# Held-back output steps after the first exponential burst, and the place of the row-sum product, in a fused attention and SwiGLU kernel

## The chip, the cores and the metric

The kernel runs on one core of one Trainium2 chip. Its time is device time in microseconds (us), the median of three executions. The profile is of one further execution. The engines are PE (TensorE, matrix products), DVE (VectorE), ACT (ScalarE), POOL (GpSimd) and SP (SyncE, which here only issues DMAs). Each of them works through its own instructions in the order in which the program has them, and semaphores hold an instruction back until what it needs is there.

## What is computed

Four batches of 12416 rows of 128 channels pass an attention over 32 inducing points, and then a gated feed-forward of width 1536:

```python
def mab(q, kv):
    s = scale * (q @ kv.transpose(0, 2, 1))
    s = s - s.max(-1, keepdims=True)
    a = np.exp(s)
    a /= a.sum(-1, keepdims=True) + 1e-09
    return a @ kv
h = mab(I, x)            # 32 rows per batch, over all 12416 rows of x
attn = mab(x, h)         # every row of x, over the 32 rows of h
g = attn @ w_gate
out = (g * sigmoid(g) * (attn @ w_val)) @ w_out
```

## The kernel before

**Columns, tiles and slots.** A batch is cut into 25 columns of 480 or 512 rows (`COLS`), and a column's feed-forward into 12 tiles of 128 hidden units (t = 0 to 11). Each batch thus has 300 slots, one per tile. In a slot the program issues a **front** (L694 and L695: two matmuls of up to 512 columns into two PSUM tiles of the six in `ps_gv`), the gate on ACT (L700, silu), the product with the value on DVE (L708), and the **split** of tiles that are due (L716 and L718: a rounded copy `h_hi`, nearly always on ACT, and the rest `h_lo`, on POOL, or on DVE for t = 1, 5 and 9). It ends with **backs** (L737 to L739: three matmuls into an accumulator `o`, of which two exist), of tiles that were fronted some slots earlier. L739 is the one that reads `h_lo`. A split is due one slot after its front where t is 1, 5 or 9, three slots after where t is 0, 4 or 8, else two. Below, "front 43" is that of slot 43 of the first batch, and "tile 40" the tile fronted in slot 40.

**Held-back steps.** `pend` lists the tiles fronted but not yet backed. After each slot, backs are issued while `pend` is longer than `ahead`. `ahead` rises by a sixth a slot up to 11 (`RAMP`, `HI`) until the last burst of the batch. In the second and third batch it rises evenly up to their first burst.

**Bursts.** In a burst slot, ACT gets a long run of exponentials with two loads of its function table around them, and PE gets all backs that the fall of `ahead` sets free: `ahead` drops to `SKEW`, which is 6, and in the first batch to 5. All tiles that wait for their split are then rounded on DVE. The first batch has a burst at slot 36 (`E0`: exponentials of its own second attention), one at slot 131 (`nxt.e1`: of the next batch's first attention) and a third later.

**The next batch's attention** is laid into the slots of the current batch by `plan`, as steps with a due slot. Steps are taken in the order of their due slots, and a step whose `acc` lists the t of the oldest held tile waits (as do all behind it). Such are the score steps `s1` (due at slots 82 and 103 here), `max_b` (110) and `hacc`, since they take one of the two `o` buffers. From slot 131 on come: the exponentials; in slot 134 three `hacc` (L323, 84 matmul passes into one `o` tile, the "hacc visit"); then `h_a` (L331, the product of the row sums), and in the next slot `h_r` and `h_b` on DVE (L335 to L337, three tiny operations on the sums, and L341, which reads the `o` tile of the visit and sets it free). The steps of the current batch's own second attention (`post`: on DVE L207, L208, L467, L475 and a rounding, on POOL L471 and L484) and leftovers of the start-up (on POOL L457) lie in fixed slots between.

The lines that decide how many steps are held:

```python
if slot < first_burst:
    ahead += (HI - ahead) / (first_burst - slot)
else:
    ahead = min(ahead + 1 / RAMP, HI) if slot < last_burst else max(ahead - 1 / RAMP, SKEW)
if slot in bursts:
    ahead = SKEW - (b == 0)
while len(pend) > ahead:
```

Of the kernel before, what the change touches and what calls it, by code (L numbers as in the profile page):

```python
# [40 lines left out]
NT = DFF // P  # L41
# [9 lines left out]
SKEW = 6  # L51

S2O = list(range(NCH - NXT, NCH)) + list(range(NCH - NXT))
NXN = 3
# [7 lines left out]
E0 = 36  # L62
# [49 lines left out]
def induced_set_attention_then_swiglu(ctx: ExitStack, tc: tile.TileContext, xt, xn, ind, wgv, wo, out):  # L112
# [58 lines left out]
    class Piece:  # L171
# [23 lines left out]
        def add(self):  # L195
            nc.gpsimd.tensor_add(out=self.w.bitcast(I32), in0=self.t.bitcast(I32), in1=self.lw.bitcast(I32))  # L196
# [365 lines left out]
    def plan(st, p):  # L562

        f, s = st.f, []

        def add(slot, step, *args):
            def go():
                f[step](*args)


            go.step = step
            go.acc = (NT - 1, 0, 1) + (2,) * (step not in ("max_b", "h_c")) if step in ("s1", "max_b", "hacc", "h_c", "s2") else ()
            s.append((slot, go))

        def blocks(q):
            return CH0[q], CH0[q] + CH[q]

        last = p["S1"][0] + p["S1"][1] * (NCH - 1)
        v1 = last - 3 * p["S1"][1]
        for q in range(NCH):  # L580
            add(p["LX"][0] + p["LX"][1] * q if q < NXT else v1 + 1 + 3 * (q - NXT), "load_xt", q)

            add(v1 if q < NXT else last, "s1", q, q not in (0, NXT))
        mb = last + p["MX"]
        add(last + 2, "max_a"), add(mb, "max_b")
        e1 = mb + p["E1"]
        for q in range(NXN):
            add(e1 - p["LN"][0] + p["LN"][1] * q, "load_xn", q)
            add(e1, "exp1_part", q)
            add(e1, "eT", q)  # L590
            add(e1 + p["HA"][q], "hacc", q, (0, NXN - 1))
        add(e1 + p["HA"][NXN - 1], "h_a")
        add(e1 + p["HA"][NXN - 1] + 1, "h_r")
        add(e1 + p["HA"][NXN - 1] + 1, "h_b")
        add(e1, "exp1_part", NXN, NCH - 1)
        for q in range(NXN, NCH):
            k = NXN + (q - NXN | 1)
            at = e1 + p["HB"][0] + p["HB"][1] * (k - NXN)
            add(max(at - p["HC"][0] - k + q, e1 + 1 + (p["HB"][0] + p["HB"][1] if q == NCH - 1 else p["HA"][0])), "load_xn", q)
            add(at - p["HC"][1] + 1 - k + q, "eT", q)  # L600
            add(at, "hacc", q, (k - 1, k))
        add(at + 1, "h_s")
        hn = at + p["HD"]
        add(hn, "h_c")
        for i, q in enumerate(S2O):
            k = i % NXT
            at = hn + 4 + p["H2"] * (NXT - 1) if i < NXT else hn + p["H2"] * (NCH - 1)
            add(at, "s2", *blocks(q), i not in (0, NXT))
            if i + NXT < NCH:
                add(at + 1, "load_xt", S2O[i + NXT])  # L610
            d = 2 if i < NXT else 1
            add(at + 1 + d * k, "s2_max", *blocks(q))
            add(at + 3 + (d + 1) * k, "s2_sub", *blocks(q))
        e2 = at + 4 + p["E2"]
        add(e2, "exp2")
        st.e1, st.bursts = e1, {e1, e2}
        for i in range(2):
            add(e2 + p["PR"][0], "proj_round", i)
            for k in range(NG * NG):
                add(e2 + p["PR"][i] + 3 + k * p["PQ"], "proj_spread", i, k // NG, k % NG)  # L620
        for q in range(NF):
            first = [u for u, (p, j) in enumerate(COLS) if p == q][0]
            s += post(st, q, nc.gpsimd, SLOTS + NT * (first - NST) + 2, SLOTS)
        return sorted(s, key=lambda x: x[0])
# [5 lines left out]
    with tc.tile_pool(name="xt0", bufs=NCH - NXT) as xt0, tc.tile_pool(name="xn0", bufs=NCH - NXN) as xn0:  # L630
# [17 lines left out]
        def run(token):  # L648
# [13 lines left out]
            e1=lambda q: f["exp1_part"](q, g=int(q >= GA)), eT=f["eT"], hq=f["hacc2"], fs=f["rescale"], su=f["sums"],  # L662
# [102 lines left out]
    for b in range(B):  # L765
        nxt = attention(b + 1, (one, oneb)[(b + 1) % 2]) if b + 1 < B else None
        if nxt is not None:
            nxt.steps = plan(nxt, PA if b == 0 else PB)
            if b == 0:
                cur.steps.append((nxt.e1, lambda: run(f"e2:52:{NTB}")))  # L770
                for q in range(2, NF):
                    base = NT * (1 + NG * (q - 1) - NST) + 2
                    base = max(base, E0 + 6) if q < 4 else max(base, nxt.e1 + 4)
                    cur.steps += post(cur, q, nc.gpsimd, base)
                cur.steps.sort(key=lambda x: x[0])
        bursts = (nxt.bursts if nxt is not None else set()) | ({E0} if b == 0 else set())
        last_burst = max(bursts, default=0)
        first_burst = min(bursts, default=0) if b else 0
        for slot in range(NT if b == 0 else 0, SLOTS):
            c, t = slot // NT, slot % NT  # L780
            u = front(cur, b, c, t)
            gate(u)
            value(u)
            left = (B - b) * SLOTS - slot
            u.cast = same if t in CAST and left > 1 else nc.scalar.copy
            u.last, u.near = left == 1, left < 3
            u.due = slot + (1 if t in DVE_TILES or left < 5 or b == 0 and slot < 2 * NT else 3 if t + 1 in DVE_TILES else 2)
            if slot in bursts:
                for w in wait + [u]:
                    w.cast = same  # L790
            for w in [w for w in wait if w.due <= slot]:
                now(w)
            wait.append(u)
            pend.append(u)
            if slot in bursts:
                while wait:
                    now(wait[0])
            for a in (cur, nxt):
                while a is not None and a.steps and a.steps[0][0] <= slot:

                    if pend and pend[0].t in getattr(a.steps[0][1], "acc", ()):
                        break
                    step = getattr(a.steps[0][1], "step", "")
                    if step == "h_c" and slot < a.hb + 3:
                        break
                    if step == "h_s":
                        a.hb = slot
                    a.steps.pop(0)[1]()
            if slot < first_burst:
                ahead += (HI - ahead) / (first_burst - slot)  # L810
            else:
                ahead = min(ahead + 1 / RAMP, HI) if slot < last_burst else max(ahead - 1 / RAMP, SKEW)
            if slot in bursts:
                ahead = SKEW - (b == 0)
            while len(pend) > ahead:
                if pend[0] in wait:
                    now(pend[0])
                back(pend.pop(0))
        if nxt is not None:
            nxt.steps = [(at - SLOTS, f) for at, f in nxt.steps]  # L820
        for u in wait:
            u.due -= SLOTS
        cur = nxt
# [45 lines left out]
```

## Time and profile before

| | us |
|---|---|
| median of three executions | 1379.59 |
| lowest and highest of the three | 1379.53, 1379.64 |
| the profiled execution | 1379.63 |
| its span, from the first to the last instruction | 1377.8 |
| PE busy, by the page | 1368.3 |
| ACT busy | 1241.5 |
| DVE busy | 1195.4 |
| POOL busy | 1180.8 |

The busy time of PE holds pipelined matmuls whose records overlap, and short waits disappear in it. Distances from start to start show what PE does: a matmul of 512 columns has a record of 380 ns, and the next one starts 216 ns later.

### The profile page before, as it was taken

Reading aid. Unit: us, or ns where it says so; the run is one execution under the profiler, and the core shown is the slowest. Engines: PE = TensorE matmul, PEld = TensorE weight load, DVE = VectorE, ACT = ScalarE, POOL = GpSimd, SP = SyncE. Lnnn points to the kernel's source line nnn. Section 1 sums busy time; section 2 is a strip of 40 time slices with the busy share of each in tenths; the row PEclk is TensorE's granted clock in tenths of the full one; section 3 lists DMA queues with packets and bytes.
Section 4 is the critical chain, followed back from the end, with each engine's and each line's share of the span. In section 5 each row is a group of like instructions: output and inputs, shape, how many; then the busy total and the mean of one; then the engine's idle time right before and its main releaser. Section 6 shows DMA issues by size and latency. Waiting matters only on the chain.

```text
span 1377.8 us, 25215 instructions
## 1 busy us (share of the span) xinstructions
PE 1368.3 (99%) x7459; PEld 1182.2 (86%) x7459; DVE 1195.4 (87%) x2088; ACT 1241.5 (90%) x2380; POOL 1180.8 (86%) x994
## 2 busy tenths in 40 slices
PE   9999999999999999999999999999999999999998
PEld 6578788889988887899998888789999888889998
DVE  6889879988988889888898888988888888888887
ACT  4989898889998888899999889799999999999998
POOL 1689868889998878899898878889989989989987
PEclk9999999999999999999999999999999999999999
DMA  9224424312144343221123523321111111111110
GB/s 365 85 85 144 147 82 142 125 46 73 41 126 154 107 142 111 64 58 44 44 69 119 178 77 112 121 72 53 44 37 45 39 47 39 39 45 38 42 44 22
DMA packets 50680, 119.49 MB, mean 87 GB/s; under 512 B 11376, under 2 KB 28272, under 8 KB 50544
## 3 DMA queue, kind: packets, MB, share of 16 engines
q1 hardware_dynamic: 50544, 117.90, 26.1%
q8 instruction: 59, 0.97, 0.3%
q14 instruction: 77, 0.63, 0.2%
HBM read 62.54 MB, written 25.43 MB: 64 GB/s over the span
## 4 chain that ended last, share of the span: by engine, by line
PE 96%; ACT 2%; DVE 1%; DMA 1%; issue 0%; SPq 0%; DVEq 0%; ACTq 0%
PE o L737 18%; PE gv L694 18%; PE gv L695 18%; PE o L738 18%; PE o L739 18%; PE gv L275 2%; PE o L323 1%; PE o L275 1%; DMA xt_sb<-xt 1%; ACT silu L700 1%; PE o L734 0%; PE gv L424 0%; PE gv L267 0%; DVE eT L313 0%; ACT xn_sb L184 0%
## 5 line engine op out<-in xcount | busy, mean ns | idle before, releaser
L718 POOL TENSOR_TENSOR h_lo<-h,h_hi 128x512 fp32r<-128x512 f32 (+1 forms) x889 | 1089.8, 1255 | 149.1 <-ACT h_hi L716 107.9
L700 ACT ACTIVATE silu<-gv 128x512 f32<-128x512 f32 (+1 forms) x1200 | 707.1, 590 | 105.2 <-PE gv L694 72.4
L708 DVE TENSOR_TENSOR h<-gv,silu 128x512 f32<-128x512 f32 (+1 forms) x891 | 588.9, 665 | 90.4 <-PE o L738 50.6
L716 ACT CAST h_hi<-h 128x512 fp32r<-128x512 f32 (+1 forms) x778 | 470.5, 605 | 0.5 <-DVE h L708 0.5
L694 PE MATMUL gv<-stack,tw 128*128 128x512 f32 (+1 forms) x1200 | 452.4, 377 | 1.6 <-DVE stack L544 1.0
L695 PE MATMUL gv<-stack,tw 128*128 128x512 f32 (+1 forms) x1200 | 448.3, 374 | 0.2 <-ACT silu L700 0.2
L737 PE MATMUL o<-h_hi,wo_lo 128*128 128x512 f32 (+1 forms) x1188 | 445.4, 375 | 0.4 <-DVE hn L341 0.4
L739 PE MATMUL o<-h_lo,wo_hi 128*128 128x512 f32 (+1 forms) x1188 | 443.0, 373 | 0.0
L738 PE MATMUL o<-h_hi,wo_hi 128*128 128x512 f32 (+1 forms) x1188 | 442.8, 373 | 0.0
L708 DVE TENSOR_TENSOR gv<-gv,silu 128x512 f32<-128x512 f32 (+1 forms) x297 | 202.4, 682 | 68.4 <-PE o L738 46.0
L694 PEld LDWEIGHTS gv<-stack,tw 128*128 128x128 f32 x1200 | 226.8, 189 | 34.6 <-ACT tw L416 3.1
L737 PEld LDWEIGHTS o<-h_hi,wo_lo 128*128 128x128 f32 x1188 | 224.5, 189 | 34.1 <-issue 10.6
L695 PEld LDWEIGHTS gv<-stack,tw 128*128 128x128 f32 x1200 | 226.7, 189 | 30.3 <-ACT silu L700 4.0
L739 PEld LDWEIGHTS o<-h_lo,wo_hi 128*128 128x128 f32 x1188 | 224.5, 189 | 24.8 <-POOL h_lo L718 0.5
L738 PEld LDWEIGHTS o<-h_hi,wo_hi 128*128 128x128 f32 x1188 | 224.6, 189 | 23.4
L718 DVE TENSOR_TENSOR h_lo<-gv,h_hi 128x512 fp32r<-128x512 f32 (+1 forms) x297 | 197.3, 664 | 0.8
L716 ACT CAST h_hi<-gv 128x512 fp32r<-128x512 f32 (+1 forms) x295 | 168.7, 572 | 7.5 <-DVE gv L708 7.0
L211 DVE TENSOR_REDUCE h_hi<-h 128x512 fp32r<-128x512 f32 (+1 forms) x113 | 73.7, 661 | 0.0
L748 DVE COPY ob<-o 128x512 f32<-128x512 f32 (+1 forms) x99 | 65.7, 664 | 0.2 <-PE o L739 0.2
L484 POOL TENSOR_TENSOR a_lo<-aT,a_hi 128x480 fp32r<-128x480 f32 (+2 forms) x26 | 30.1, 1159 | 0.0
L196 POOL TENSOR_TENSOR wgv_sb<-s_all 128x512 int32<-128x512 int32 x2 | 2.9, 1492 | 28.8 <-ACT s_all L184 28.8
L471 POOL TENSOR_TENSOR s_all<-s_all,sm 128x512 f32<-128x512 f32 (+2 forms) x27 | 26.1, 965 | 0.0
(156 smaller groups left out, 480.9 us busy)
## 6 DMA issues: line engine op xcount, KB each, us to landing
xt_sb<-xt SPq DMA_DIRECT2D x32, 896.0 KB, 5.0
xn_sb<-xn SPq DMA_DIRECT2D x18, 896.0 KB, 5.6
out<-ob SPq DMA_DIRECT2D x52, 256.0 KB, 2.0
out<-ob SPq DMA_DIRECT2D x48, 240.0 KB, 2.0
stack<-a_hi SPq DMA_DIRECT2D x96, 64.0 KB, 2.0
stack<-a_lo SPq DMA_DIRECT2D x96, 64.0 KB, 2.0
stack<-a_hi SPq DMA_DIRECT2D x96, 60.0 KB, 2.0
stack<-a_lo SPq DMA_DIRECT2D x96, 60.0 KB, 2.0
```

Source lines behind the costliest of these rows:

```text
L211: nc.vector.tensor_reduce(out=out, in_=in_.unsqueeze(2), op=ALU.max, axis=AX.X)
L275: nc.tensor.matmul(out=ps[32 * j:32 * j + 32, 32 * (lo - b0):32 * (hi - b0)], lhsT=lhsT, rhs=st.xt[q][:, lo - CH0[q]:hi - CH0[q], j, :], s ...
L694: nc.tensor.matmul(out=u.g[:, :n], lhsT=st.w[:, wcol(0, t)], rhs=rhs, start=True, stop=True)
L695: nc.tensor.matmul(out=u.v[:, :n], lhsT=st.w[:, wcol(1, t)], rhs=rhs, start=True, stop=True)
L700: nc.scalar.activation(out=u.s[:, :u.n], in_=u.g[:, :u.n], func=AF.Silu)
L708: nc.vector.tensor_mul(out=u.h[:, :n], in0=u.v[:, :n], in1=u.s[:, :n])
L716: u.cast(out=u.hi[:, :n], in_=u.h[:, :n])
L718: eng.tensor_sub(out=u.lo[:, :n], in0=u.h[:, :n], in1=u.hi[:, :n].bitcast(F32))
L737: nc.tensor.matmul(out=o[:, :n], lhsT=wo_lo[:, ws], rhs=hi, start=(t == 0), stop=False)
L738: nc.tensor.matmul(out=o[:, :n], lhsT=wo_hi[:, ws], rhs=hi, start=False, stop=False)
L739: nc.tensor.matmul(out=o[:, :n], lhsT=wo_hi[:, ws], rhs=lo, start=False, stop=(t == NT - 1))
L748: (nc.scalar.copy if u.last else nc.vector.tensor_copy)(out=ob[:, :n], in_=o[:, :n])
```

## The change

Three things change. In the first batch, the burst at slot 36 leaves four steps held back instead of five. From the slot after it, `ahead` rises evenly so that it reaches 11 just ahead of slot 131, instead of by a sixth a slot, which reached 11 at slot 73. And in the batches' `plan`, `h_a` comes ahead of the three `hacc` of its visit and gets their `acc` list, and `h_r` and `h_b` fall due in the slot of the visit instead of the one behind it.

```diff
--- before.py
+++ after.py
@@ -569,7 +569,7 @@
 
 
             go.step = step
-            go.acc = (NT - 1, 0, 1) + (2,) * (step not in ("max_b", "h_c")) if step in ("s1", "max_b", "hacc", "h_c", "s2") else ()
+            go.acc = (NT - 1, 0, 1) + (2,) * (step not in ("max_b", "h_c")) if step in ("s1", "max_b", "h_a", "hacc", "h_c", "s2") else ()
             s.append((slot, go))
 
         def blocks(q):
@@ -584,14 +584,14 @@
         mb = last + p["MX"]
         add(last + 2, "max_a"), add(mb, "max_b")
         e1 = mb + p["E1"]
+        add(e1 + p["HA"][0], "h_a")
         for q in range(NXN):
             add(e1 - p["LN"][0] + p["LN"][1] * q, "load_xn", q)
             add(e1, "exp1_part", q)
             add(e1, "eT", q)
             add(e1 + p["HA"][q], "hacc", q, (0, NXN - 1))
-        add(e1 + p["HA"][NXN - 1], "h_a")
-        add(e1 + p["HA"][NXN - 1] + 1, "h_r")
-        add(e1 + p["HA"][NXN - 1] + 1, "h_b")
+        add(e1 + p["HA"][NXN - 1], "h_r")
+        add(e1 + p["HA"][NXN - 1], "h_b")
         add(e1, "exp1_part", NXN, NCH - 1)
         for q in range(NXN, NCH):
             k = NXN + (q - NXN | 1)
@@ -806,12 +806,14 @@
                     if step == "h_s":
                         a.hb = slot
                     a.steps.pop(0)[1]()
+            if b == 0 and slot == E0 + 1:
+                first_burst = nxt.e1
             if slot < first_burst:
                 ahead += (HI - ahead) / (first_burst - slot)
             else:
                 ahead = min(ahead + 1 / RAMP, HI) if slot < last_burst else max(ahead - 1 / RAMP, SKEW)
             if slot in bursts:
-                ahead = SKEW - (b == 0)
+                ahead = SKEW - (b == 0) - (b == 0 and slot == E0)
             while len(pend) > ahead:
                 if pend[0] in wait:
                     now(pend[0])
```

**PE, slots 43 to 46 of the first batch.** The rows up to the back of tile 40, whose halves are `h_hi_1279` before and `h_hi_1285` now (gv_1303 and gv_1317 are fronts 45 and 46 before; gv_1277 and gv_1293 are fronts 43 and 44 now). Before:

```order
L694 MATMUL gv_1303<-stack_824,tw_546 128x512
L695 MATMUL gv_1304<-stack_824,tw_546 128x512
L737 MATMUL o_1252<-h_hi_1248,wo_lo_114 128x512
L738 MATMUL o_1252<-h_hi_1248,wo_hi_113 128x512
L739 MATMUL o_1252<-h_lo_1249,wo_hi_113 128x512
L694 MATMUL gv_1317<-stack_824,tw_546 128x512
L695 MATMUL gv_1318<-stack_824,tw_546 128x512
L737 MATMUL o_1252<-h_hi_1279,wo_lo_114 128x512
L738 MATMUL o_1252<-h_hi_1279,wo_hi_113 128x512
L739 MATMUL o_1252<-h_lo_1280,wo_hi_113 128x512
```

Now:

```order
L694 MATMUL gv_1277<-stack_824,tw_546 128x512
L695 MATMUL gv_1278<-stack_824,tw_546 128x512
L737 MATMUL o_1241<-h_hi_1252,wo_lo_114 128x512
L738 MATMUL o_1241<-h_hi_1252,wo_hi_113 128x512
L739 MATMUL o_1241<-h_lo_1253,wo_hi_113 128x512
L694 MATMUL gv_1293<-stack_824,tw_546 128x512
L695 MATMUL gv_1294<-stack_824,tw_546 128x512
L737 MATMUL o_1241<-h_hi_1285,wo_lo_114 128x512
L738 MATMUL o_1241<-h_hi_1285,wo_hi_113 128x512
L739 MATMUL o_1241<-h_lo_1286,wo_hi_113 128x512
```

The back of tile 40 stood behind front 46 and stands behind front 44.

**PE, slots 129 to 131.** The fronts of these slots are gv_2715, gv_2729 and gv_2747 before, and gv_2718, gv_2735 and gv_2747 now. Before:

```order
L694 MATMUL gv_2715<-stack_2230,tw_546 128x512
L695 MATMUL gv_2716<-stack_2230,tw_546 128x512
L737 MATMUL o_2573<-h_hi_2585,wo_lo_114 128x512
L738 MATMUL o_2573<-h_hi_2585,wo_hi_113 128x512
L739 MATMUL o_2573<-h_lo_2586,wo_hi_113 128x512
L694 MATMUL gv_2729<-stack_2230,tw_546 128x512
L695 MATMUL gv_2730<-stack_2230,tw_546 128x512
L737 MATMUL o_2573<-h_hi_2599,wo_lo_114 128x512
L738 MATMUL o_2573<-h_hi_2599,wo_hi_113 128x512
L739 MATMUL o_2573<-h_lo_2600,wo_hi_113 128x512
L694 MATMUL gv_2747<-stack_2230,tw_546 128x512
L695 MATMUL gv_2748<-stack_2230,tw_546 128x512
```

Now:

```order
L694 MATMUL gv_2718<-stack_2239,tw_546 128x512
L695 MATMUL gv_2719<-stack_2239,tw_546 128x512
L737 MATMUL o_2561<-h_hi_2602,wo_lo_114 128x512
L738 MATMUL o_2561<-h_hi_2602,wo_hi_113 128x512
L739 MATMUL o_2561<-h_lo_2603,wo_hi_113 128x512
L694 MATMUL gv_2735<-stack_2239,tw_546 128x512
L695 MATMUL gv_2736<-stack_2239,tw_546 128x512
L694 MATMUL gv_2747<-stack_2239,tw_546 128x512
L695 MATMUL gv_2748<-stack_2239,tw_546 128x512
```

Front 131 followed front 130 behind a back, and now follows it at once. The seven backs of the burst stand behind it in both.

**PE and DVE at the hacc visit, slot 134.** On PE (`sum` is the column of row sums, from ACT):

```order
 L695 MATMUL gv<-stack,tw 128x512
+L331 MATMUL gv<-sum_2434,fold 128x4
 L323 MATMUL o<-xn_sb,eT 32x128 x42
-L331 MATMUL gv<-sum_2428,fold 128x4
 L737 MATMUL o<-h_hi,wo_lo 128x512
```

On DVE, where the L708 row is the product of slot 135, and L207 and L208 are `post` steps:

```order
 L718 TENSOR_TENSOR h_lo<-gv,h_hi 128x512
+L335 TENSOR_REDUCE r_2878<-gv 128x1
+L336 TENSOR_SCALAR r_2878<-r_2878 128x1
+L337 RECIPROCAL r_2878<-r_2878 128x1
+L341 TENSOR_SCALAR hn<-o,r_2878 128x128
 L708 TENSOR_TENSOR h<-gv,silu 128x512
 L207 TENSOR_REDUCE pairs<-s_all 128x15
 L208 TENSOR_REDUCE sm<-pairs 128x15
-L335 TENSOR_REDUCE r_2896<-gv 128x1
-L336 TENSOR_SCALAR r_2896<-r_2896 128x1
-L337 RECIPROCAL r_2896<-r_2896 128x1
-L341 TENSOR_SCALAR hn<-o,r_2896 128x128
```

L331 moves ahead of the visit's 42 products, and the four DVE operations move ahead of the product of slot 135 and two `post` steps. The second and third batch have the same move of L331; there the four operations move ahead of one product.

On ACT and POOL no instruction changes its place. On SP, three issues of an output column move ahead of the eight or one issues that stood in front of them.

## Rows read from the trace of the kernel before

**Rows 1.** The page: busy time of the engines; the granted clock of PE in 40 slices, in tenths of full speed; the shares of the chain that ended last, by engine.

```profile
PE 1368.3 (99%) x7459; PEld 1182.2 (86%) x7459; DVE 1195.4 (87%) x2088; ACT 1241.5 (90%) x2380; POOL 1180.8 (86%) x994
...
PEclk9999999999999999999999999999999999999999
...
PE 96%; ACT 2%; DVE 1%; DMA 1%; issue 0%; SPq 0%; DVEq 0%; ACTq 0%
```

**Rows 2.** Timeline of PE, slots 33 to 51 of the first batch. Columns: start, length, engine, line, operation, names, shape, and in brackets idle time before it and what ended it. 79.81 and 81.97 are fronts 33 and 35; 83.28 is the first back of the burst; 89.22 is front 40; 96.68 is the L739 of tile 40; 98.94 is front 49; 100.34 is the second matmul of front 50; 104.24 is front 51.

```profile
79.81 0.38 PE L694 MATMUL gv<-stack,tw 128*128 128x512 f32 x1
...
81.97 0.38 PE L694 MATMUL gv<-stack,tw 128*128 128x512 f32 x1
...
83.28 0.38 PE L737 MATMUL o<-h_hi,wo_lo 128*128 128x512 f32 x1
...
89.22 0.48 PE L694 MATMUL gv<-stack,tw 128*128 128x512 f32 x1
...
96.68 0.48 PE L739 MATMUL o<-h_lo,wo_hi 128*128 128x512 f32 x1
...
98.94 0.48 PE L694 MATMUL gv<-stack,tw 128*128 128x512 f32 x1 [0.23 <-DVE h L708]
...
100.34 0.38 PE L695 MATMUL gv<-stack,tw 128*128 128x512 f32 x1
...
104.24 0.38 PE L694 MATMUL gv<-stack,tw 128*128 128x512 f32 x1
```

**Rows 3.** Timeline of ACT, the same stretch. 88.56 is the silu of slots 37 and 38, 91.38 the rounding of tile 38, 94.16 the silu of slot 43, 94.65 the rounding of tile 40, 104.71 the silu of slot 51.

```profile
88.56 1.08 ACT L700 ACTIVATE silu<-gv 128x512 f32<-128x512 f32 x2
...
91.38 0.63 ACT L716 CAST h_hi<-h 128x512 fp32r<-128x512 f32 x1
...
94.16 0.60 ACT L700 ACTIVATE silu<-gv 128x512 f32<-128x512 f32 x1
94.65 0.62 ACT L716 CAST h_hi<-h 128x512 fp32r<-128x512 f32 x1
...
104.71 0.60 ACT L700 ACTIVATE silu<-gv 128x512 f32<-128x512 f32 x1 [2.21 <-PE gv L694]
```

**Rows 4.** Timeline of POOL. The L718 rows are the `h_lo` of tiles 38 and 39 (92.09), 40 and 42 (95.34), 48 (105.89), 50 (108.38), and 51, 52, 54, 55 and 56 (109.98).

```profile
92.09 2.53 POOL L718 TENSOR_TENSOR h_lo<-h,h_hi 128x512 fp32r<-128x512 f32 x2 [1.93 <-ACT h_hi L716]
95.34 2.52 POOL L718 TENSOR_TENSOR h_lo<-h,h_hi 128x512 fp32r<-128x512 f32 x2 [0.72 <-ACT h_hi L716]
97.82 1.05 POOL L471 TENSOR_TENSOR s_all<-s_all,sm 128x512 f32<-128x512 f32 x1
...
105.89 1.29 POOL L718 TENSOR_TENSOR h_lo<-h,h_hi 128x512 fp32r<-128x512 f32 x1 [2.00 <-ACT h_hi L716]
107.13 1.29 POOL L484 TENSOR_TENSOR a_lo<-aT,a_hi 128x512 fp32r<-128x512 f32 x1
108.38 1.29 POOL L718 TENSOR_TENSOR h_lo<-h,h_hi 128x512 fp32r<-128x512 f32 x1
109.62 0.41 POOL L457 TENSOR_TENSOR s_all<-s_all,mx2b 128x128 f32<-128x128 f32 x1
109.98 6.29 POOL L718 TENSOR_TENSOR h_lo<-h,h_hi 128x512 fp32r<-128x512 f32 x5
```

**Rows 5.** Timeline of PE, front 79.

```profile
131.90 0.38 PE L694 MATMUL gv<-stack,tw 128*128 128x512 f32 x1
132.26 0.48 PE L695 MATMUL gv<-stack,tw 128*128 128x512 f32 x1
```

**Rows 6.** Timeline of PE from front 131 to front 144: 194.37 is the first matmul of front 131, 201.70, 208.32 and 215.02 are the second ones of fronts 134, 138 and 144, and 209.08 is the first back of a column, which takes the `o` buffer of the hacc visit.

```profile
194.37 0.38 PE L694 MATMUL gv<-stack,tw 128*128 128x512 f32 x1
...
201.70 0.38 PE L695 MATMUL gv<-stack,tw 128*128 128x512 f32 x1
...
208.32 0.38 PE L695 MATMUL gv<-stack,tw 128*128 128x512 f32 x1
209.08 0.45 PE L737 MATMUL o<-h_hi,wo_lo 128*128 128x512 f32 x1 [0.38 <-DVE hn L341]
...
215.02 0.48 PE L695 MATMUL gv<-stack,tw 128*128 128x512 f32 x1
```

**Rows 7.** Timeline of ACT from slot 130: the silu of slots 130 and 131, the end of the row sums, the silu of slot 142.

```profile
193.70 0.60 ACT L700 ACTIVATE silu<-gv 128x512 f32<-128x512 f32 x1
...
194.84 0.60 ACT L700 ACTIVATE silu<-gv 128x512 f32<-128x512 f32 x1
...
201.68 0.19 ACT L307 ACTIVATION_READ_ACCUMULATOR s_all<-s_all,negmax 128x1 f32 x1
...
214.34 0.62 ACT L700 ACTIVATE silu<-gv 128x512 f32<-128x512 f32 x1
```

**Rows 8.** Timeline of DVE: the products of slots 135 and 136.

```profile
206.62 0.69 DVE L708 TENSOR_TENSOR h<-gv,silu 128x512 f32<-128x512 f32 x1
...
208.85 0.68 DVE L708 TENSOR_TENSOR h<-gv,silu 128x512 f32<-128x512 f32 x1
```

**Rows 9.** Timeline of ACT at the second batch's hacc visit: the end of the row sums.

```profile
486.45 0.19 ACT L307 ACTIVATION_READ_ACCUMULATOR s_all<-s_all,negmax 128x1 f32 x1
```

**Rows 10.** Timeline of PE at the same place: the second matmul of the front in that slot.

```profile
486.55 0.38 PE L695 MATMUL gv<-stack,tw 128*128 128x512 f32 x1
```

**Rows 11.** Timeline of PE at the start: a wait of the first front.

```profile
37.25 0.48 PE L694 MATMUL gv<-stack,tw 128*128 128x512 f32 x1 [1.02 <-DVE stack L544]
```

## Prediction

> **What bounds the kernel now.** The page comes first: PE is on 96% of the chain that ended last, and its granted clock is full in all slices [rows 1]. So the time is PE's own work plus the moments in which PE waits, and the change adds and removes no matmul. Hence everything is decided by waits of PE, and these I read from start to start in PE's timeline: fronts 33 and 35 are ten matmuls and 2.16 us apart, so a matmul costs 0.216 us, a front 0.431, a back 0.647, a slot with one back 1.08 [rows 2]. What a stretch takes beyond its count of matmuls is waiting. After a wait the next start comes some 0.10 us late as well: L739 of tile 40 starts at 96.68, and the next front 0.32 later, at 97.00, instead of 0.22; I add 0.10 to each wait.
>
> From the burst's first back (83.28) to the end of front 50 (100.34 + 0.22 = 100.56) are 17.28 us [rows 2]. In it are 14 fronts and 15 backs, 73 matmuls, 15.74 us. So 1.54 us were lost behind the first burst, in short waits such as those at fronts 40 and 49, for PSUM that ACT and DVE held. Two more places matter: front 79 lost 0.14 + 0.10 [rows 5], and the first back behind the hacc visit waited from 208.54 to 209.08 for its `o` buffer, 0.54 + 0.08 [rows 6]. These 2.4 us are all that the change can win.
>
> **How far a back has to stand behind its front.** This is what the first part of the change touches. The way of a tile whose split is due three slots later goes through the front of that third slot: front to its silu 0.47 (104.24 to 104.71), silu to the rounding of the older tile 0.49 (94.16 to 94.65), rounding to `h_lo` on POOL 0.69 (94.65 to 95.34), `h_lo` to L739 1.34 (95.34 to 96.68) [rows 2 to 4]. Sum: 2.99 us from the start of that front. The order on ACT and POOL is unchanged, so this way stays.
>
> **Slots 37 to 50: four held.** Now PE stands closer. The back of tile 40 follows front 44, so from front 43 to its L739 there are nine matmuls, 1.94 us, where the way needs 2.99: a wait of 1.05 + 0.10. Tile 44 has the same (its back follows front 48, its split belongs to slot 47): 1.15 again. Both include what smaller waits for tiles 39 and 43 lie in the same stretch. Tile 38 is a third: the burst delays the silu of slots 37 and 38 to 88.56 in either version, and with it the rounding (91.38) and `h_lo` (92.09) of tile 38, so its L739 can't start before 92.09 + 1.34 = 93.43 [rows 3, 4]. PE would be there 44 matmuls after 83.28, at 92.77: 0.66 + 0.10. In sum 3.06 us of new waits. The 1.54 of old ones go: PE has one back more ahead of front 37 and is late enough afterwards for the PSUM to be free. Net **+1.5**.
>
> **Slots 51 to 57: five held, and POOL is full.** The nearest row is POOL's run from 105.89: `h_lo` of 48, `a_lo`, `h_lo` of 50, a subtraction of 0.36, then five more without a gap [rows 4]. It started 1.65 behind front 51 (104.24), and `h_lo` of 52 started 1.26 into the last row, at 111.24, 7.00 behind that front; its L739 can start at 8.34. Before, this back stood behind front 61 and waited for nothing. Now it stands behind front 57: 34 matmuls, 7.33, and 0.10 for the restart behind the scores in slot 50. The wait is 0.91 + 0.10: **+1.0**. From then on POOL's lead regrows with the held steps; I find 0.05 to 0.16 of room at tiles 56 and 60, so from nothing to 0.3 more.
>
> **Slots 74 to 80.** The old order came here with ACT late from the steep rise, the new one doesn't: the 0.24 at front 79 go, **-0.25**.
>
> **The second burst, slot 131.** The even rise skips a back in slot 130, so front 131 comes 0.43 behind front 130 instead of 1.08. ACT needs 0.98 for a silu and a rounding, so the silu of slot 131, behind which the burst stands, starts some 0.97 behind front 131 instead of 0.47 (194.37 to 194.84) [rows 6, 7]: 0.5 later by PE's clock. The row sums ended at 201.68 + 0.19 = 201.87 and would now end at 202.37. L331, which now leads the visit, could start when front 134 is through, 201.70 + 0.22 = 201.92: it waits 0.45, and 84 passes of L323 and every front are queued behind it. That wait alone is not the cost. Before, PE lost 0.54 at the `o` buffer and then waited again until front 144, at 215.02, for the silu of slot 142 at 214.34 [rows 6, 7]. That silu hangs on ACT and DVE, and through them on the burst. So the stretch ends when they end: 0.45 to 0.5 later, **+0.45**.
>
> **The move of `h_a`, `h_r` and `h_b`.** DVE frees the `o` buffer one product and two steps earlier, so the 0.62 at 209.08 go. But the product of slot 136 (208.85 before) still stands behind the same DVE work: the four small operations only change places with the product of slot 135 (206.62) and the two steps [rows 8]. ACT's later silus follow the product of slot 136, so PE meets the same silu of slot 142: gain 0 to 0.1, in the 0.45 above. In the second batch the row sums end at 486.64 and PE is free for L331 at 486.77 [rows 9, 10]; the third is alike. I take 0 and keep 0 to 0.1 for each. The SP issues that change places wait for the same copies and have slots to spare: 0.
>
> **Sum**, against the profiled execution's own 1379.63 (span 1377.8 and 1.8 around it; the median is 1379.59): 1.5 + 1.0 - 0.25 + 0.45 = +2.7, that is **1382.3 us**. Each term is good to some 0.2 and their sum to 0.6, the POOL term most uncertain: 1381.7 to 1382.9.
>
> **Rivals.**
> - *The old waits go and no new ones come* (it ends on the faster side). The waits behind the burst are ACT's, the extra back and the gentler rise are what ACT lacks, and the pieces of POOL arrive in time. Then 1.54 + 0.25 + 0.62 go: 1377.2. It holds if `h_lo` of tile 40 is there within 1.94 of front 43. For it: nearly all waits in that stretch name ACT or DVE. Against it: L739 of tile 40 started at once when `h_lo` was there even with six held [rows 2, 4]. 7%.
> - *Only the first stretch costs.* PE's new waits give POOL and ACT time, POOL comes to slot 51 ahead, and the silu of slot 131 is not late. Then +1.5 - 0.25: 1380.9. Against it: the POOL run starts anew behind front 51 in any case. 18%.
> - *POOL doesn't get its lead back.* The room at tiles 56 and 60 is missing, tiles up to 66 wait as well, and L331 waits in the second and third batch: +2.7 + 0.5 + 0.3 + 0.1, 1383.3. 17%.
> - *The clock falls.* Behind the first burst PE gets three waits of a microsecond within 20 us. The first front waited 1.02 us [rows 11] amid other waits, and the clock stayed at the upper level, 2.4 GHz [rows 1]. If it fell to 1.2 in slots 42 to 57, some 80 matmuls would take 0.216 longer: 17 us, 1399. 1%. The Trainium skill, TensorE: Matmul & The Clock Gate, section What's actually happening, has the throttled clock as the default state that activity releases, which speaks against adding waits; by that rule alone this case would weigh more, and the trace, with longer waits at a full clock, bears it out in nothing.
>
> That the change doesn't do what it says is no rival: the order on PE shows it.
>
> **How the numbers follow.** The forecast has 57%. A measurement of this kernel can tell some 0.2%, 2.76 us, from no change, so slower begins at 1382.35, just above the forecast. Of the forecast's 57% I put 25 above that line and 32 below; the POOL rival adds 16 above and the clock 1; the first-stretch rival lies within; of the first one 3 at most go below 1376.9. Slower 0.42, same 0.55, faster 0.03. The range for 8 in 10 holds the forecast, most of the second and third rival, and leaves the first and the clock out: 1380.2 to 1383.7.
>
> **What would show it.** Right: L739 of tiles 38, 40 and 44 with waits for POOL `h_lo`, each 0.7 to 1.1; a further microsecond for POOL between fronts 51 and 58; L331 of the first batch waiting some 0.45 for the row sums; no wait for `hn`; front 144 still waiting for silu; fronts 40 and 79 without waits. Wrong: no waits for POOL in slots 42 to 49 (then the way from front to L739 is shorter than I read, and the time falls), or front 144 reached without waiting (then the second burst cost nothing and the move of `h_a` won its 0.6).

## The result and the profile of the changed kernel

The changed kernel takes 1389.87 us, the median of six executions (1388.26 to 1390.08). The kernel before takes 1379.62 beside it (six executions, 1379.03 to 1380.31). The ratio is 1.0071, with a 95% interval of 1.006 to 1.0082: slower by 10 us, where +2.7 was forecast, and outside the range.

The profiled execution took 1390.08, with a span of 1388.2. Its page, in the lines that answer to [rows 1]:

```profile
PE 1371.5 (99%) x7459; PEld 1185.3 (85%) x7459; DVE 1196.1 (86%) x2088; ACT 1241.3 (89%) x2380; POOL 1180.2 (85%) x994
...
PEclk9999999999999999999999999999999999999999
...
PE 92%; ACT 4%; issue 1%; POOL 1%; DVE 1%; DMA 1%; SPq 0%; POOLq 0%; DVEq 0%; ACTq 0%
```

PE does the same work, and its share of the chain falls from 96 to 92%, with ACT's doubled. The view that groups PE's waits (what waits, for what, us in total, times, longest) names two places. Its first two rows:

```profile
PE gv L331 <- ACT silu L700: 5.5, 3, 2.2
PE o L739 <- POOL h_lo L718: 1.9, 4, 0.7
```

The second row was predicted. The first was not: L331, three times. Here is PE's timeline around it, from front 134 of the first batch, and then the same place in the second and the third batch:

```profile
203.73 0.38 PE L694 MATMUL gv<-stack,tw 128*128 128x512 f32 x1
203.94 0.38 PE L695 MATMUL gv<-stack,tw 128*128 128x512 f32 x1
206.55 0.41 PE L331 MATMUL gv<-sum,fold 128*128 128x4 f32 x2 [2.23 <-ACT silu L700]
206.88 4.18 PE L323 MATMUL o<-xn_sb,eT 128*32 128x128 f32 x84
211.00 0.48 PE L737 MATMUL o<-h_hi,wo_lo 128*128 128x512 f32 x1
...
491.89 0.38 PE L695 MATMUL gv<-stack,tw 128*128 128x512 f32 x1
493.93 0.39 PE L331 MATMUL gv<-sum,fold 128*128 128x4 f32 x2 [1.66 <-ACT silu L700]
494.24 2.60 PE L323 MATMUL o<-xn_sb,eT 128*32 128x128 f32 x84
...
828.56 0.38 PE L695 MATMUL gv<-stack,tw 128*128 128x512 f32 x1
830.60 0.39 PE L331 MATMUL gv<-sum,fold 128*128 128x4 f32 x2 [1.66 <-ACT silu L700]
830.91 4.26 PE L323 MATMUL o<-xn_sb,eT 128*32 128x128 f32 x84
```

L331 reads only the row sums, and yet it waits for a silu. Start to start, each wait cost 2.61, 2.04 and 2.04, less the 0.216 that a matmul takes: 2.39, 1.82 and 1.82. The second thing to see is the length of L323: 84 passes took 2.60 in the second batch, as before, but 4.18 and 4.26 in the first and third. The table of stretches (from and to; length; PE busy and its matmuls; granted clock; DMA) tells why:

```profile
196.00:206.00 10.00, 8.32 (x39) 1.00 0.07 27
206.00:211.00 5.00, 4.45 (x86) 0.66 0.02 3
211.00:216.00 5.00, 5.00 (x25) 1.00 0.00 0
493.00:498.00 5.00, 4.08 (x92) 1.00 0.34 91
830.00:835.00 5.00, 4.40 (x86) 0.66 0.32 89
835.00:840.00 5.00, 5.00 (x27) 1.00 0.75 278
```

A granted clock of 0.66 behind the first and the third wait, between stretches at 1.00: part of the time it was at its lower level, 1.2 GHz. L323 took 1.58 and 1.66 longer there. The forty slices of the page don't show it, since one slice is 35 us long.

ACT's rows of the first batch show which silu it is. 202.65 is the second last of the row sums, 204.40 the last; 205.90 are the silus of slots 132 and 133:

```profile
202.65 0.19 ACT L307 ACTIVATION_READ_ACCUMULATOR s_all<-s_all,negmax 128x1 f32 x1
202.75 1.75 ACT L307 ACTIVATE s_all<-s_all,negmax 128x1760 f32<-128x1760 f32 x1
204.40 0.19 ACT L307 ACTIVATION_READ_ACCUMULATOR s_all<-s_all,negmax 128x1 f32 x1
204.60 1.28 ACT L700 ACT_TABLE_LOAD   x1
205.90 1.08 ACT L700 ACTIVATE silu<-gv 128x512 f32<-128x512 f32 x2
```

The last row sum is there at 204.59. PE could start L331 at 203.94 + 0.22 = 204.16, so the sums account for 0.43, as predicted. The rest of the wait is a table load and the silu of slot 132. The same two silus of the second and the third batch show it again:

```profile
493.27 1.09 ACT L700 ACTIVATE silu<-gv 128x512 f32<-128x512 f32 x2
...
829.95 1.09 ACT L700 ACTIVATE silu<-gv 128x512 f32<-128x512 f32 x2
```

In all three batches L331 starts 0.65 or 0.66 behind the start of this row, and one silu takes some 0.6.

**The buffer theory.** L331 writes into a tile of its own from `ps_gv` (lines 328 to 330). That pool has six, and every front takes two. Fronts 132, 133 and 134 take all six, so the tile for L331 is the one that front 132's gate lies in, and it is free only when ACT has read it. ACT reads it behind the whole burst. Before, the three hacc stood ahead of L331 and used up 2.5 us on PE, and by then the silu was through (it started at 203.18, and L331 at 204.54). The same rotation holds in the other batches.

**Rivals.** The *late-burst theory*: the even rise leaves out a back ahead of slot 131, so the burst and all behind it come late, and the place of `h_a` is harmless. The *row-sum theory*: L331 waits for what it reads.

### The profile page after: what moved, and what is told of

Same layout as the page of the kernel before. It is cut to its first block, busy times and chain, and to the rows that moved or that the text cites. A ratio compares the mean times of both kernels' runs of the same rounds, so it can differ in the third digit from the quotient of the medians.

```text
span 1388.2 us, 25214 instructions
## 1 busy us (share of the span) xinstructions
PE 1371.5 (99%) x7459; PEld 1185.3 (85%) x7459; DVE 1196.1 (86%) x2088; ACT 1241.3 (89%) x2380; POOL 1180.2 (85%) x994
## 4 chain that ended last, share of the span: by engine, by line
PE 92%; ACT 4%; issue 1%; POOL 1%; DVE 1%; DMA 1%; SPq 0%; POOLq 0%; DVEq 0%; ACTq 0%
PE gv L694 18%; PE gv L695 17%; PE o L737 17%; PE o L739 17%; PE o L738 17%; PE gv L275 2%; PE o L323 2%; ACT silu L700 1%; PE o L275 1%; ACT s_all L307 1%; POOL h_lo L718 1%; DMA xt_sb<-xt 1%; PE o L734 0%; ACT L700 0%; ACT h_hi L716 0%
## 5 line engine op out<-in xcount | busy, mean ns | idle before, releaser
L718 POOL TENSOR_TENSOR h_lo<-h,h_hi 128x512 fp32r<-128x512 f32 (+1 forms) x889 | 1089.0, 1252 | 160.2 <-ACT h_hi L716 111.9
L708 DVE TENSOR_TENSOR h<-gv,silu 128x512 f32<-128x512 f32 (+1 forms) x891 | 589.1, 665 | 90.5 <-PE o L738 53.1
L695 PE MATMUL gv<-stack,tw 128*128 128x512 f32 (+1 forms) x1200 | 447.8, 373 | 0.2 <-ACT silu L700 0.2
L739 PE MATMUL o<-h_lo,wo_hi 128*128 128x512 f32 (+1 forms) x1188 | 443.8, 374 | 2.0 <-POOL h_lo L718 1.9
L708 DVE TENSOR_TENSOR gv<-gv,silu 128x512 f32<-128x512 f32 (+1 forms) x297 | 202.3, 681 | 74.4 <-PE o L738 50.7
L737 PEld LDWEIGHTS o<-h_hi,wo_lo 128*128 128x128 f32 x1188 | 224.5, 189 | 34.3 <-issue 10.5
L695 PEld LDWEIGHTS gv<-stack,tw 128*128 128x128 f32 x1200 | 226.8, 189 | 28.0 <-ACT silu L700 2.2
L739 PEld LDWEIGHTS o<-h_lo,wo_hi 128*128 128x128 f32 x1188 | 224.5, 189 | 29.4 <-POOL h_lo L718 5.4
L718 DVE TENSOR_TENSOR h_lo<-gv,h_hi 128x512 fp32r<-128x512 f32 (+1 forms) x297 | 197.1, 664 | 0.7
L471 POOL TENSOR_TENSOR s_all<-s_all,sm 128x512 f32<-128x512 f32 (+2 forms) x27 | 26.0, 963 | 0.0
```

The source lines that it names most:

```text
L695: nc.tensor.matmul(out=u.v[:, :n], lhsT=st.w[:, wcol(1, t)], rhs=rhs, start=True, stop=True)
L708: nc.vector.tensor_mul(out=u.h[:, :n], in0=u.v[:, :n], in1=u.s[:, :n])
L718: eng.tensor_sub(out=u.lo[:, :n], in0=u.h[:, :n], in1=u.hi[:, :n].bitcast(F32))
L737: nc.tensor.matmul(out=o[:, :n], lhsT=wo_lo[:, ws], rhs=hi, start=(t == 0), stop=False)
L739: nc.tensor.matmul(out=o[:, :n], lhsT=wo_hi[:, ws], rhs=lo, start=False, stop=(t == NT - 1))
```

## Experiments

Each kernel was timed in five rounds beside the kernel before, whose medians in the three sets were 1379.41, 1379.44 and 1379.64. "The plan part" below is the change to `acc` and `plan`, "the first-batch part" the change to `ahead`.

### One part at a time

**Only the plan part.** The old kernel with the first two hunks of the diff.

```diff
...
+        add(e1 + p["HA"][0], "h_a")
...
-        add(e1 + p["HA"][NXN - 1], "h_a")
-        add(e1 + p["HA"][NXN - 1] + 1, "h_r")
-        add(e1 + p["HA"][NXN - 1] + 1, "h_b")
+        add(e1 + p["HA"][NXN - 1], "h_r")
+        add(e1 + p["HA"][NXN - 1], "h_b")
```

> The old kernel with only the move of h_a (and of h_r and h_b); the first batch's held-back steps as before. Buffer theory: L331 takes a ps_gv buffer that the gate tile of front 132 (of the matching front in batches 2 and 3) still holds, its silu stands on ACT behind the burst, and PE now reaches L331 some 1.8 us too early in each of three visits. Three waits of 1.8 us named ACT silu, 5.4, less 0.6 for the hn wait and up to 0.9 given back later: +4 without a fall of the granted clock, +1.7 more for each visit at half clock (L323 4.2 us instead of 2.6): 1383.5 to 1389, likeliest two falls, 1387. Late-burst theory (the even rise skips a back ahead of slot 131, and that makes the burst late): no wait of over 0.5 at L331, 1379.2 to 1380.2. Row-sum theory: 0 to 0.2 at each L331, 1379.0 to 1380.2.

Measured: 1385.82 (five executions, 1384.43 to 1387.18), ratio 1.0041 (1.0027 to 1.0054). PE's timeline, with all three visits:

```profile
203.74 0.39 PE L331 MATMUL gv<-sum,fold 128*128 128x4 f32 x2 [1.74 <-ACT silu L700]
204.06 2.60 PE L323 MATMUL o<-xn_sb,eT 128*32 128x128 f32 x84
...
489.61 0.39 PE L331 MATMUL gv<-sum,fold 128*128 128x4 f32 x2 [1.66 <-ACT silu L700]
489.92 2.60 PE L323 MATMUL o<-xn_sb,eT 128*32 128x128 f32 x84
...
826.56 0.39 PE L331 MATMUL gv<-sum,fold 128*128 128x4 f32 x2 [1.67 <-ACT silu L700]
826.88 4.26 PE L323 MATMUL o<-xn_sb,eT 128*32 128x128 f32 x84
```

The waits are there without the even rise, so the late-burst theory falls as the cause of all three. It has a share in the first: 1.90 here from start to start (L695 before it starts at 201.62), against 2.39 in the changed kernel, so 0.49 are the even rise's. In the profiled execution, 1385.91, the clock fell in the third visit alone (0.64 from 826 to 830). The five times lie in three groups, 1384.4 to 1384.6, 1385.8 to 1385.9, and 1387.2. I read them as no fall, one and two; only the middle one has a profile.

**Only the first-batch part.** The old kernel with the last hunk.

```diff
+            if b == 0 and slot == E0 + 1:
+                first_burst = nxt.e1
...
-                ahead = SKEW - (b == 0)
+                ahead = SKEW - (b == 0) - (b == 0 and slot == E0)
```

> The old kernel with only the first-batch part: four steps held after slot 36 and the even rise. h_a behind the hacc as before. Buffer theory: the stretches of slots 36 to 131 cost the 2.4 us that the changed kernel shows there, the three hacc cover the wait for the silu, the clock stays full: 1381.8 to 1382.6. Late-burst theory: the visit of batch 1 costs 4 us here as well, 1385 to 1387.

Measured: 1381.90, ratio 1.0017 (1.0008 to 1.0026), with a full clock. So the first-batch part costs 2.5 by itself, and L331, behind the hacc, waits for nothing.

### The same order without the `ps_gv` tile

**The changed kernel, with L331 in the visit's own `o` tile.** The matrix product of the hacc fills columns 0 to 127 of that tile; L331 takes four columns behind them, and `h_a`, which now comes first, takes the tile in place of the first hacc. Everything else is the changed kernel.

```diff
-            if q == group[0]:
+            if q == group[0] and q:
                 st.hps = ps_o.tile([P, 512], F32, name="o")
...
         def h_a():
-            st.hp = ps_gv.tile([P, 512], F32, name="gv")
+            st.hps = ps_o.tile([P, 512], F32, name="o")
+            st.hp = st.hps[:, C:C + NXN + 1]
```

> The changed kernel, but h_a writes into four free columns of the visit's own o tile and takes no ps_gv buffer; it still leads the three hacc. Buffer theory: what is left at L331 is the row sums, 0.45 in batch 1 and 0 to 0.1 in the others, the clock stays full, 1381.6 to 1382.8 (the time that was predicted for the change). Row-sum theory: the waits of 2.2 and 1.7 us stay, and with them the falls of the clock, 1388 to 1390. Late-burst theory: only batch 1 keeps its loss, 1384 to 1386.

Measured: 1382.38, ratio 1.002 (1.0011 to 1.0029). The first visit (L332 is L331 moved by a line), and the row of ACT with the silus of slots 132 and 133:

```profile
204.82 0.38 PE L696 MATMUL gv<-stack,tw 128*128 128x512 f32 x1
205.52 0.38 PE L332 MATMUL o<-sum,fold 128*128 128x4 f32 x2 [0.32 <-ACT s_all L307]
205.83 2.60 PE L323 MATMUL o<-xn_sb,eT 128*32 128x128 f32 x84
```

```profile
206.78 1.09 ACT L701 ACTIVATE silu<-gv 128x512 f32<-128x512 f32 x2
```

This settles it. The product now starts 1.26 ahead of the silus that it waited for. With the order unchanged and only the buffer taken away, 7.5 us go (7.3 when each kernel is taken against the kernel before beside it). What L331 now waits for is the row sums, 0.32 idle and 0.48 from start to start; in the other two batches it waits for nothing. The clock is full.

**The old kernel with the plan part and the `o` tile.** Both edits above, without the first-batch part.

> The old kernel with h_a ahead of the hacc in the o tile and h_r and h_b in the slot of the visit; the first batch as before. Buffer theory: no waits at L331 over 0.3, the 0.4 of the hn wait gone, and what it wins is given back at the next silu: 1379.0 to 1379.8. Row-sum theory: 1383 to 1389 as the first kernel.

Measured: 1379.06, ratio 0.9997 (0.9988 to 1.0005). The hn wait of [rows 6] is gone, and the two matmuls of front 141 then wait for DVE and for a silu instead, 0.07 and 0.31, with 0.10 for the restart: all but 0.07 of what was won is given back within six slots, as predicted.

The differences in the start of a front, against the profiled execution of before and with the difference at slot 36 taken off, put the five kernels side by side (slots counted from the start of the first batch):

| at slot | changed | plan part | first-batch part | changed, `o` tile | plan part, `o` tile |
|---|---|---|---|---|---|
| 131 (second burst) | 2.39 | -0.01 | 2.39 | 2.40 | -0.01 |
| 135 (behind the visit) | 6.39 | 1.89 | 2.39 | 2.88 | -0.01 |
| 145 | 5.56 | 1.07 | 2.78 | 2.81 | -0.07 |
| 386 | 5.49 | 1.09 | 2.71 | 2.95 | -0.14 |
| 388 (second visit) | 7.31 | 2.91 | 2.71 | 2.87 | -0.22 |
| 686 | 7.00 | 2.88 | 2.41 | 2.56 | -0.53 |
| 688 (third visit) | 10.49 | 6.37 | 2.41 | 2.49 | -0.61 |

Between slots 388 and 686 four of the five lose 0.3 less than the kernel before, all of it at fronts 636 and 637. Among them are the kernel with only the first-batch part and one without it, so neither part is needed for that; the cause is open.

### How much of the hacc covers the wait

**`h_a` behind the first of the three hacc**, and **behind two of them**, on the old kernel with `h_r` and `h_b` in the slot of the visit and `h_a` in the `acc` list (the number is 0, and 1 for the second kernel):

```diff
             add(e1 + p["HA"][q], "hacc", q, (0, NXN - 1))
+            if q == 0:
+                add(e1 + p["HA"][q], "h_a")
```

> The old kernel with h_a behind the first of the three hacc and ahead of the other two; h_r and h_b in the slot of the visit. The L331 of the kernel with only h_a's move waited 1.7 us in each batch; one hacc covers 0.83 of that, so each waits 0.8 to 0.95. If a wait costs only itself: +2.5, less 0.5 for the hn wait, 1380.8 to 1382. If shorter waits let the granted clock fall just the same, 1.4 to 1.7 more for each visit: 1383 to 1386. If L331 doesn't wait for the buffer: 1379.0 to 1379.6.

> The old kernel with h_a behind two of the three hacc; h_r and h_b in the slot of the visit. Buffer theory: each hacc covers some 0.85 us of the wait (1.7 with none ahead, 0.7 with one), so with two ahead it is 0 to 0.1 and the clock stays full: 1378.9 to 1379.5. Without that theory (the first hacc's effect was another) a wait of about 0.7 stays: 1381 to 1381.6.

Measured: 1381.45, ratio 1.0014 (1.0005 to 1.0022), and 1379.98, ratio 1.0003 (0.9994 to 1.0012). First visits, of the one and then of the other:

```profile
201.75 1.07 PE L323 MATMUL o<-xn_sb,eT 128*32 128x128 f32 x28
203.56 0.39 PE L331 MATMUL gv<-sum,fold 128*128 128x4 f32 x2 [0.74 <-ACT silu L701]
203.87 1.74 PE L323 MATMUL o<-xn_sb,eT 128*32 128x128 f32 x56
```

```profile
201.84 1.74 PE L323 MATMUL o<-xn_sb,eT 128*32 128x128 f32 x56
203.65 0.39 PE L331 MATMUL gv<-sum,fold 128*128 128x4 f32 x2
203.97 1.07 PE L323 MATMUL o<-xn_sb,eT 128*32 128x128 f32 x28
```

The wait is 1.74, 0.74 and next to nothing, with none, one and two hacc ahead: it ends at a fixed time, and PE's own work uses it up. In the second kernel a rest of it is left: the silus of slots 132 and 133 start at 203.00, and L331 again 0.65 behind them.

```profile
203.00 1.08 ACT L701 ACTIVATE silu<-gv 128x512 f32<-128x512 f32 x2
```

This kernel came out above its expected 1378.9 to 1379.5. Its visit is 3.43 from the second matmul of front 134 to the next back, against 3.08 before, so 0.35 longer. The rest of the wait makes 0.14 of them (L331 starts 0.34 behind the last pass ahead of it, and 0.20 before). The other 0.2 come with the cut through the run of hacc; why is open.

**Only `h_r` and `h_b` one slot earlier**, `h_a` last as it was:

```diff
-        add(e1 + p["HA"][NXN - 1] + 1, "h_r")
-        add(e1 + p["HA"][NXN - 1] + 1, "h_b")
+        add(e1 + p["HA"][NXN - 1], "h_r")
+        add(e1 + p["HA"][NXN - 1], "h_b")
```

> The old kernel with h_a behind the three hacc as it was, and only h_r and h_b brought forward to the slot of the visit. If what the lead was good for lies in these two alone: the hn wait of 0.54 goes, PE then meets the silu that ended the stretch anyway, 1378.9 to 1379.5. Rival (the lead of h_a itself helps, since h_r can then run while the hacc do): h_r now starts only behind them, the hn wait stays at 0.2 to 0.5, 1379.3 to 1379.8.

Measured: 1379.20, ratio 0.9998 (0.9989 to 1.0006). `hn` is written at 207.21, and the back that needs the buffer starts at 208.63 without waiting. So the hn wait goes by these two lines alone, and the lead of `h_a` was needed for nothing.

### The first-batch part taken apart

**Four held, but the old rise**, and **five held, then the even rise**: each has one of the two edits of the last hunk.

> The old kernel with four steps held after slot 36, but the old rise by a sixth a slot; h_a as before. POOL-chain theory (a back needs 2.99 us from the third front behind its tile's own): no back is left out before slot 42, where it now is, so tile 40 is backed behind front 45 (14 matmuls, 3.02 us: no wait), and only tile 38 still waits some 0.2; the steps held in slots 51 to 57 are six and seven, so nothing waits there. New waits 0.2 to 0.4 in all, the old 1.54 go in part: 1378.2 to 1379.7. Rival (four held are too few for POOL whatever the rise): the waits of 0.5, 0.8 and 0.8 stay, 1380.5 to 1382.

> The old kernel with five steps held after slot 36 as before, and then the even rise to slot 131. POOL-chain theory: every tile is backed five or more slots behind its front, tile 52 six, so no wait for h_lo over 0.1; the waits at fronts 40 and 41 stay, those of slots 45 to 49 (0.8) go in part, and the burst at slot 131 is late as in the changed kernel, under the hacc: 1378.7 to 1379.8. Rival (the even rise is what costs, since POOL has no lead in slots 51 to 57): +0.7 to +1.2 there, 1380.1 to 1381.

Measured: 1380.45, ratio 1.0009 (1.0 to 1.0017), and 1380.34, ratio 1.0006 (0.9997 to 1.0014). Neither did what I expected of it. In the first, tile 40 is backed behind front 45, and its L739 still waits 0.82 (start to start); another microsecond comes in slots 72 to 80, where the steep rise meets ACT (front 80 waits 0.47 for a silu). In the second, the same back waits 0.54, L739 in slot 57 waits 0.39, and the hn wait grows from 0.54 to 0.93 since the burst is late. The first back of the burst and the L739 of tile 40, in the changed kernel and then in these two:

```profile
83.12 0.38 PE L737 MATMUL o<-h_hi,wo_lo 128*128 128x512 f32 x1
...
96.57 0.48 PE L739 MATMUL o<-h_lo,wo_hi 128*128 128x512 f32 x1 [0.65 <-POOL h_lo L718]
```

```profile
83.56 0.38 PE L737 MATMUL o<-h_hi,wo_lo 128*128 128x512 f32 x1
...
96.95 0.48 PE L739 MATMUL o<-h_lo,wo_hi 128*128 128x512 f32 x1 [0.65 <-POOL h_lo L718]
```

```profile
83.18 0.38 PE L737 MATMUL o<-h_hi,wo_lo 128*128 128x512 f32 x1
...
96.58 0.48 PE L739 MATMUL o<-h_lo,wo_hi 128*128 128x512 f32 x1 [0.37 <-POOL h_lo L718]
```

They are 13.45, 13.39 and 13.40 apart, and 96.68 - 83.28 = 13.40 before [rows 2]. So behind the burst the piece of tile 40 comes when ACT and POOL get to it. How many steps are held only decides how much other work PE has until then.

**Tiles 40 and 44 split one slot sooner**, with the first-batch part:

```diff
-... 3 if t + 1 in DVE_TILES else 2)
+... 3 if t + 1 in DVE_TILES and not (b == 0 and slot in (40, 44)) else 2)
```

> The kernel with only the first-batch part (four held and the even rise), but tiles 40 and 44 are split two slots after their front instead of three; h_a as in the old kernel. POOL-chain theory: their rounding on ACT comes 0.4 to 0.6 sooner, and the waits of L739 of tiles 40 and 44 (0.81 and 0.82) shrink by 0.4 to 0.8 each, if nothing else on POOL holds their h_lo: 1380.3 to 1381.2. Rival (POOL is busy with other pieces there, so that a sooner rounding finds it occupied): the waits stay, 1381.6 to 1382.2.

Measured: 1380.90, ratio 1.001 (1.0002 to 1.0019), 1.0 less than the first-batch part alone. (One of the twelve executions took 6765.74, and why is not known; the other eleven took 1380.79 to 1381.17.) L739 of tile 40 starts 12.63 behind the burst and waits 0.06 instead of 0.81. Tile 44 hardly waits either, but PE now comes sooner to tile 43, whose `h_lo` stands on POOL behind L471 (which starts at 97.74), and waits 0.90 there in slot 47 instead of 0.14. One of the two waits went, and the other only passed to a neighbour.

### Two tries at a faster kernel

The plan part with the `o` tile, and the old rise started three and six slots later (k is 3, then 6):

```diff
-                ahead = min(ahead + 1 / RAMP, HI) ...
+                ahead = min(ahead + (b > 0 or not E0 < slot <= E0 + k) / RAMP, HI) ...
```

> A try at a faster kernel: h_a leads in the o tile as in the fourth kernel, five held after slot 36, and the rise by a sixth starts three slots later, so that the first back is left out in slot 45 instead of 42. If tile 40's back is bound by ACT's time behind the burst (it then starts no earlier than 13.4 us behind the burst's first back in any order), tile 40 still comes behind front 46, no h_lo wait over 0.1, and the waits of 0.7 at slots 45 to 49 shrink, since PE is no longer ahead of ACT there: 1378.2 to 1379.0. Rival (later steps then lack a held step and wait for h_lo in slots 47 to 57): 1379.1 to 1380.

> As the kernel with the rise three slots later, but six slots later, so that the first back is left out in slot 48 and tile 40 comes behind front 45. If tile 40's back is bound by ACT's time: it waits the 0.5 that the kernel with five held and the even rise showed there, and the waits at slots 45 to 49 go: 1378.7 to 1379.4. Rival as there: 1379.5 to 1380.3.

Measured: 1379.84, ratio 1.0001 (0.9992 to 1.0009), and 1380.50, ratio 1.0006 (0.9998 to 1.0015). Both missed. With three slots, the waits of slots 45 to 49 fall from 0.75 to 0.47, and front 52 then waits for a silu, 0.48 and 0.10, and fronts 73 to 79 lose 1.14 instead of 0.29. With six, L739 of tile 40 waits 0.54, about the 0.5 that was expected, and fronts 74 to 80 lose 1.33 instead of 0.28, again with a wait for a silu. What the rival named, waits for `h_lo` in slots 47 to 57, came to 0.10 at most. No kernel here can be told from the one before as faster.

## Why the prediction was wrong

**The step that failed** is the price of `h_a`'s move: "In the second batch the row sums end at 486.64 and PE is free for L331 at 486.77 [rows 9, 10]; the third is alike. I take 0". In the first batch the same reading gave 0.45. It asked when the data that L331 reads is there, and not when the buffer that it writes is free. In its place the runs showed 1.66 to 2.23 us of idle PE in each of the three visits, and behind it 1.6 more where the clock fell, and they went with the buffer alone (1389.87 to 1382.38). The trace of before held the answer: its ACT rows at the two visits that the prediction used have the silu of slot 132 not before 203.18, and its counterpart in the second batch not before 487.94, while PE was free for L331 at 201.92 and 486.77.

```profile
203.18 1.09 ACT L700 ACTIVATE silu<-gv 128x512 f32<-128x512 f32 x2
...
487.94 1.09 ACT L700 ACTIVATE silu<-gv 128x512 f32<-128x512 f32 x2
```

The silu takes some 0.6, so waits of 1.86 and 1.77 could be read off, and the kernel with only the plan part has 1.90 and 1.82 from start to start (1.74 and 1.66 idle).

**The clock** had 1%, in slots 42 to 57 and with 17 us. It did not fall there, behind three waits of up to 0.82. It fell behind L331, for 1.6 us a time. Two of the six executions took 1388.3, at a mean clock of 0.999, the other four 1389.9 to 1390.1, at 0.997 or 0.998. The profiled one, 1390.08, has two falls; the 1.6 less of the first two fits one, but they have no profile. The page cited there (the Trainium skill, TensorE: Matmul & The Clock Gate, section What's actually happening) has the throttled state as the default which activity releases. Here the trace agrees, with a clock of 0.66 over the five us from 206 behind 2.23 us without work. Behind the 1.66 us of the second batch the clock stayed at 1.00. So a fall came, but neither where the rival had it nor of its size.

**The first-batch part** was right. Forecast for slots 37 to 131: 1.5 + 1.0 - 0.25 = 2.25; measured 2.39 in three kernels, and 2.5 by the medians. In pieces: from the first back at 83.12 to the end of front 50, 103.93 + 0.22, are 21.03, with 14 fronts and 18 backs, 82 matmuls or 17.68 in it, so 3.35 lost instead of 1.54: +1.8 for the 1.5 forecast. Waits of L739 stood where they were named, tile 38 at 93.27 (0.52), tile 40 at 96.57 (0.81) and tile 44 at 102.31 (0.82), for 0.66, 1.05 and 1.05 forecast; tile 43 and the roundings of slot 48 made up the rest. In slots 55 to 57 they were 0.22, 0.41 and 0.06, 0.99 with the restarts, for 1.0. Fronts 40 and 79 wait no more.

```profile
93.27 0.48 PE L739 MATMUL o<-h_lo,wo_hi 128*128 128x512 f32 x1 [0.36 <-POOL h_lo L718]
...
96.57 0.48 PE L739 MATMUL o<-h_lo,wo_hi 128*128 128x512 f32 x1 [0.65 <-POOL h_lo L718]
...
102.31 0.48 PE L739 MATMUL o<-h_lo,wo_hi 128*128 128x512 f32 x1 [0.66 <-POOL h_lo L718]
```

One idea in it was too narrow: "from front 43 to its L739" 2.99 us. In the changed kernel it is 93.59 to 96.57, 2.98. But with the old rise, one more slot of distance did not remove the wait. Right behind a burst the way starts at ACT's own backlog and not at the front.

**The second burst and the hn wait** were right: the row sums alone cost 0.48 in the kernel with the `o` tile (0.45 forecast), and taking the hn wait away won 0.6 for six slots and 0.07 from there on. By the end its profiled execution is 0.61 ahead, half of it at fronts 636 and 637; the medians (ratio 0.9997, 0.9988 to 1.0005) show no gain. The changed kernel with the `o` tile, 1382.38, is the change as I had read it, at 1382.3.

The sum of the changed kernel, from the table: 2.4 to slot 131; 2.4 and 1.6 at the first visit; 0.9 given back; 1.8 at the second; 0.3 less at fronts 636 and 637; 1.8 and 1.7 at the third: 10.5.

## What to carry to other kernels

Before an instruction is moved forward, list what it writes as well as what it reads: with a rotating pool of six tiles, its buffer is the one of the sixth allocation back, and its release is read from the row of the engine that empties it. Work that stands ahead of an instruction may be covering a wait that the trace therefore doesn't show, and the first row to look at is the engine with the longest run ahead of it. A small result can take free columns of a tile that its visit holds anyway; here that was worth 7.3 to 7.5 us.

## What the runs showed of the hardware

The granted clock fell to its lower level behind single idle times of 2.23, 1.66 and 1.67 us on a PE that was else fully busy, and did not fall behind others of 1.74, 1.66 and 1.66; behind the waits of 0.74, 0.67 and 0.66 at L331 in the kernel with one hacc ahead it stayed at full, and behind the 1.02 of [rows 11], in the kernel before, it was 1.00 from 37 to 46. At 1.66 both happened within one execution, in the second and in the third batch of the changed kernel. Each fall lengthened the 84 passes of L323 from 2.60 to 4.18 or 4.26. What decides it at 1.7 is open, and waits between 1.02 and 1.66 were not tried.
